# The front of a hand-written list of steps put in another order, with twelve more products of zeros, in a gated-attention and feed-forward kernel

## Chip, cores and metric

The kernel runs on one core of one Trainium2 chip. The metric is the device time of one execution in microseconds (us). Three runs of the kernel before took 465.76, 466.92 and 478.84 us, median 466.92 us.

## What is computed

The first half is a gated linear attention (an mLSTM cell) over 4 batches, 8 heads, 768 time steps and a head size of 40; the second is a feed-forward layer with a piecewise square between two matrix products, over 3072 tokens, 320 model columns and 2048 hidden ones.

```python
for t in range(S):
    m_new = np.maximum(f_gate[:, :, t] + m, i_gate[:, :, t])
    f_stab = np.exp(f_gate[:, :, t] + m - m_new)
    i_stab = np.exp(i_gate[:, :, t] - m_new)
    C = f_stab[:, :, None, None] * C + i_stab[:, :, None, None] * np.einsum('bhd,bhe->bhde', vt, kt)
    n = f_stab[:, :, None] * n + i_stab[:, :, None] * kt
    h_tilde = np.einsum('bhde,bhe->bhd', C, qt)
    y[:, :, t] = o * h_tilde / denom
...
h = x @ w_in
g = np.where(pos, h, np.where(neg, 0.0, (h + beta) ** 2 / (4.0 * beta)))
return (g @ w_out).astype(np.float32)
```

## The kernel before

**Tiles.** Time is cut into six chunks of 128 steps. A block is one chunk of one batch with its 8 heads, 24 blocks in all, numbered n = 4 * chunk + batch; blocks 0 to 3 are the first chunk, which has no state to carry in. Four blocks make one tile of 512 tokens for the feed-forward half, and that half runs in 96 groups (six tiles by 16 slices of 128 hidden columns).

**A block.** `score` (line 668) multiplies keys by queries on TensorE into two PSUM banks, and VectorE multiplies each half with the block's decay matrix. `main` (line 739) multiplies that by the block's values, which GpSimd has scaled by a gate before (`scale1`, line 660, step `v1`), divides, applies the output gate, transposes on TensorE and writes the tile `xh`, `xl`. `carry` (line 717) makes the state that the next chunk needs, from values scaled by another gate (`scale2`, line 711, step `v2`). For the first chunk the decay matrix is built on TensorE: `mask` (line 453) puts a triangle into PSUM and `add` (line 462) adds the running sums `ac` of the gates; `dec` takes the exponential on ScalarE. For blocks 0 to 3, `scale1` and `scale2` write over the block of values that they read (lines 663 to 665, 713).

**Gates.** `sums` scans the first chunk's gates on VectorE, `gtail` and `gex` finish them. For chunks 1 to 4 together, `bmax` scans 512 steps (`m_r`), sends the rows to other partitions through four transfers (`m_b`, line 308), and `bsum`, `btail`, `exps` go on from there.

**Weights.** `W.0`, `W.1`, ... load pieces of `w_in` and `w_out` in turn (line 502); steps `w` convert a piece on ScalarE (`mg`, `win`, `wh`) and VectorE (`win`, `wl`). `mm.g` is the first product of group g, `out`, `outh`, `outl` the second.

**Zeros.** `hot.k` (line 547) is k products of 512 columns of zeros, which nobody reads:

```python
def hot(k):
    out = psum_a()
    for _ in range(k):
        nc.tensor.matmul(out, zeros[:, :P], zeros, start=True, stop=True)
```

**What sets the order.** One list of step names, `STEPS` (line 48), is walked from left to right (lines 920 to 954). Every call of an engine goes through `InOrder` (line 175), which makes each engine execute its instructions in the order of that walk; so nearly all records of the profile bear line 189, and tiles tell them apart. All loads go through one queue, SP's, in the order of the list. PSUM has eight banks, shared by everything (line 543). Where a name stands several times (`score.1 ... score.1`), each mention runs the next part of that step.

Of the kernel before, what the change touches and what calls it, by code (L numbers as in the profile page):

```python
# [48 lines left out]
    "fi.0 mask.1 fb.0 W.0 vv.0 mask.0 hot.2 sums.0 mask.3 qk.1 add.1 hot.2 add.0 qk.2 w.0 w.0 bmax.0 id.0 dec.1.0 "  # L49
    "dec.1.1 dec.0.0 score.1 qk.3 gtail.0 hot.2 hot.2 bmax.0 gex.0 score.1 mask.2 qk.0 add.2 dec.2.0 dec.2.1 vv.2 "  # L50
    "add.3 v.4 dec.3.1 v1.1 dec.3.0 score.1 og.0 W.1 dec.0.1 score.2 main.1 score.0 bsum.0 bsum.0 bsum.0 w.0 "
    "score.3 score.2 score.2 one.0 score.0 v.1 score.0 v1.2 btail.0 w.0 v1.0 sig.0 main.1 btail.0 hot.4 btail.0 "
    "btail.0 w.0 v1.3 main.0 score.3 v.0 main.0 W.2 hot.2 exps.0 main.0 main.1 main.2 hot.2 hot.2 qn.5 A.4 score.3 "
    "v2.4 main.2 main.2 main.0 w.1 v2.1 qk.4 main.0 w.1 cs.0 main.3 main.1 main.2 main.0 W.3 v.5 carry.4 main.3 "
    "main.3 hot.2 v2.0 qn.4 main.1 decs.0 main.1 v.2 w.1 carry.1 main.3 A.5 A.6 main.2 w.2 carry.0 main.2 main.3 "
    "main.3 prep.4 carry.0 w.2 v1.4 prep.4 v2.5 score.4 w.2 prep.4 decs.0 W.4 carry.1 w.3 -- score.4 mm.0 relu.0 "
    "max.0 mm.1 w.2 main.4 w.2 relu.1 main.4 W.5 carry.5 W.6 carry.4 v2.2 w.3 w.3 main.5 main.5 prep.5 prep.5 "
    "score.4 carry.2 carry.2 max.1 mm.3 relu.3 prep.5 mm.2 w.4 carry.5 qk.5 prep.6 main.4 relu.2 main.4 v1.5 max.3 "
    "w.4 w.4 carry.5 prep.6 w.5 qk.6 og.1 max.2 out.0 out.1 out.2 w.5 w.5 w.4 w.4 score.5 so.1 score.5 score.5 A.7 "
    "W.7 score.6 w.6 carry.4 carry.4 v.6 w.6 prep.7 score.6 prep.6 mm.5 w.6 score.6 v1.6 qn.6 sig.1 main.5 main.4 "  # L60
    "main.4 so.2 relu.5 so.2 max.5 main.5 mm.4 relu.4 w.6 main.5 w.6 qn.7 w.7 w.7 prep.7 out.3 main.6 main.6 main.6 "
    "v2.6 carry.6 max.4 mm.6 carry.5 w.7 gh.5 gl.5 carry.6 gh.4 so.3 so.3 v.3 v2.3 carry.3 W.8 outh.4.2.3 carry.6 "
    "w.8 w.8 mm.7 outh.4.0.1 gl.4 main.6 outl.4 outh.5.2.3 A.8 relu.6 carry.3 main.7 A.9 qk.7 score.7 w.8 main.5 "
    "prep.9 relu.7 max.6 max.7 main.6 gh.6 gl.6 W.9 outh.5.0.1 outl.5 outh.6.2.3 outh.6.0.1 w.9 W.10 W.11 outl.6 "
    "w.9 w.9 v.8 main.7 w.8 w.8 v.7 score.7 W.12 prep.7 score.7 w.10 w.10 w.10 qk.9 gh.7 lg.0 main.4 main.4 gl.7 "
    "main.4 mm.9 relu.9 max.9 qn.8 mm.8 v1.7 main.7 carry.6 W.13 w.11 w.11 w.11 v2.7 carry.7 W.14 w.10 w.10 main.6 "
    "relu.8 carry.7 max.8 carry.7 gh.9 outh.7.0.1 main.7 w.12 w.12 w.12 outh.7.2.3 so.4 so.4 mm.11 relu.11 mm.10 "
    "main.8 prep.8 main.7 v.9 w.12 main.5 w.12 outl.7 gh.8 outh.8.0.1 outh.8.2.3 main.5 main.5 gl.8 qn.9 w.13 w.13 "
    "gl.9 mm.12 w.13 relu.10 max.10 max.11 w.14 w.14 so.1 w.14 so.5 so.5 gh.10 relu.12 gl.10 max.12 main.7 outl.8 "
    "outh.9.2.3 qk.8 outh.9.0.1 outl.9 mm.13 relu.13 gh.11 main.8 max.13 w.14 gl.11 w.14 W.15 w.15 outh.10.2.3 "  # L70
    "outh.10.0.1 outl.10 main.6 main.6 main.6 so.6 carry.7 so.6 w.15 w.15 v1.8 og.2 ++ gh.13 qk.10 gh.12 gl.12 "
    "score.8 prep.8 score.8 gl.13 outh.11.0.1 A.10 main.8 main.8 main.7 main.7 main.7 outh.11.2.3 outl.11 mm.15 "
    "relu.15 max.15 outh.12.0.1 outh.12.2.3 outl.12 prep.8 outh.13.2.3 so.7 score.8 main.8 main.8 mm.14 v2.8 "
    "relu.14 max.14 gh.14 mm.17 relu.17 main.9 main.9 mm.16 v2.9 so.7 outh.13.0.1 outl.13 outh.14.2.3 stack.10 "
    "max.17 gh.17 qk.10 score.9 carry.8 stack.10 prep.10 qn.10 gl.14 outh.14.0.1 outl.14 gl.17 prep.9 prep.9 mm.19 "
    "score.9 score.9 carry.8 qn.11 so.0 so.0 carry.8 gh.15 relu.16 max.16 gl.15 relu.19 max.19 v1.9 carry.8 main.9 "
    "qk.11 stack.11 stack.11 A.11 prep.11 qk.12 main.9 main.9 main.8 gh.19 main.8 gl.19 outh.15.2.3 sig.2 stack.10 "
    "stack.10 outh.15.0.1 outl.15 sto.0.1 sto.0.3 gh.16 gl.16 mm.20 relu.20 max.20 qk.11 main.8 main.8 mm.22 "
    "relu.22 max.22 sto.0.2 carry.9 carry.9 mm.18 relu.18 max.18 main.9 mm.25 mm.23 main.10 main.10 prep.10 prep.10 "
    "v.10 relu.25 score.10 score.10 main.9 main.9 outh.16.2.3 v.11 outh.16.0.1 outl.16 outh.17.0.1 qk.12 gh.18 "  # L80
    "gl.18 outh.17.2.3 outl.17 carry.9 sto.0.0 stack.11 outh.18.0.1 score.10 stack.11 v.13 outh.18.2.3 outl.18 "
    "outh.19.2.3 qn.13 main.9 gh.22 prep.11 main.8 max.25 v2.10 carry.10 v1.10 mm.21 main.10 main.8 A.12 main.8 "
    "gh.20 carry.9 gl.20 relu.23 mm.27 main.10 main.10 main.10 A.14 qk.14 carry.10 max.23 outh.19.0.1 outl.19 "
    "outh.20.0.1 outh.20.2.3 relu.21 max.21 gl.22 main.9 gh.21 gl.21 score.11 score.11 main.10 prep.11 score.11 "
    "main.10 main.10 stack.12 stack.12 main.11 mm.24 relu.24 stack.12 v1.11 main.11 main.11 main.11 main.11 max.24 "
    "gh.23 gl.23 qk.13 mm.26 relu.26 max.26 main.11 outl.20 outh.21.0.1 gh.26 main.10 mm.31 relu.31 stack.12 "
    "outh.21.2.3 qn.12 A.13 gh.25 max.31 gh.24 gl.24 stack.14 outl.21 prep.12 prep.12 carry.10 main.9 main.9 v.12 "
    "outh.22.0.1 outh.22.2.3 outl.22 carry.10 qk.13 outh.23.2.3 outh.23.0.1 outl.23 main.11 main.11 mm.29 gl.25 "
    "outh.24.0.1 relu.29 v2.11 outh.24.2.3 main.11 mm.28 main.11 gl.26 outl.24 main.10 carry.11 max.29 qn.14 "
    "relu.27 max.27 gh.31 prep.13 prep.12 outh.25.0.1 outh.25.2.3 outl.25 relu.28 stack.14 main.9 main.10 max.28 "  # L90
    "main.10 gh.27 gl.27 outh.26.0.1 main.11 main.11 main.11 stack.13 v2.12 v1.12 outh.26.2.3 main.12 main.12 "
    "main.12 gh.29 gl.29 main.13 main.13 carry.11 mm.30 score.12 outl.26 outh.27.0.1 score.12 score.12 stack.13 "
    "prep.13 prep.13 stack.13 gl.31 main.12 main.12 gh.28 gl.28 relu.30 mm.35 outh.27.2.3 outl.27 carry.12 "
    "outh.28.0.1 prep.14 carry.11 carry.11 mm.32 outh.28.2.3 outl.28 outh.29.0.1 outh.29.2.3 main.12 main.12 v.15 "
    "outl.29 v1.13 max.30 og.3 prep.14 stack.13 score.13 relu.32 gh.30 qk.15 outh.30.2.3 max.32 gl.30 v2.13 A.15 "
    "prep.14 carry.12 carry.12 main.12 relu.35 qk.14 max.35 gh.35 sig.3 qn.15 gh.32 outh.30.0.1 score.13 g5.5 "
    "score.13 main.13 main.13 main.13 main.13 outl.30 outh.31.0.1 outh.31.2.3 outl.31 stack.15 stack.15 mm.36 "
    "relu.36 v.14 gl.35 mm.33 sto.1.3 carry.13 v2.14 relu.33 max.33 mm.34 carry.12 max.36 gh.33 qk.15 gl.32 mm.39 "
    "main.15 qn.16 carry.13 carry.13 A.16 gl.33 sto.1.0 relu.34 qk.16 main.13 sto.1.1 relu.39 max.34 main.13 g5.5 "
    "carry.13 stack.15 stack.15 mm.41 g5.5 gh.34 outh.32.0.1 outh.32.2.3 outl.32 outh.33.2.3 outh.33.0.1 relu.41 "  # L100
    "max.41 stack.14 gh.36 outl.33 outh.34.2.3 outh.34.0.1 qk.17 prep.15 max.39 prep.15 gh.39 carry.14 mm.38 "
    "relu.38 main.12 gl.36 sto.1.2 gl.34 mm.37 outl.34 outh.35.2.3 outh.35.0.1 main.13 main.13 relu.37 main.15 g5.5 "
    "carry.14 v.18 v1.14 outl.35 outh.36.2.3 outh.36.0.1 main.14 stack.14 score.14 gl.39 main.12 max.37 gh.37 qk.16 "
    "mm.40 mm.43 max.38 qk.17 v2.15 main.14 stack.16 carry.15 main.14 score.14 stack.16 outl.36 score.14 gl.37 "
    "outh.37.2.3 outh.37.0.1 relu.40 outl.37 prep.15 main.14 main.14 relu.43 main.14 max.40 score.15 main.14 max.43 "
    "gh.38 gl.38 score.15 score.15 main.12 carry.14 main.14 stack.17 outh.38.0.1 outh.38.2.3 outl.38 gh.40 gl.40 "
    "main.12 main.12 stack.16 stack.16 prep.16 main.13 main.13 main.13 stack.17 prep.16 v1.15 prep.16 mm.45 g5.5 "
    "carry.14 mm.42 relu.42 mm.47 main.15 outh.39.0.1 main.14 max.42 v.16 gh.41 gl.41 qk.18 main.15 main.15 qn.17 "
    "outh.39.2.3 mm.44 stack.17 outl.39 outh.40.2.3 outh.40.0.1 outl.40 outh.41.2.3 relu.47 main.15 max.47 carry.15 "
# [919 lines left out]
```

## Time and profile before

| | us |
|---|---|
| median of three runs | 466.92 |
| lowest and highest run | 465.76, 478.84 |
| profiled execution, its own time | 465.84 |
| its span in the trace | 464.1 |
| TensorE (PE) busy | 456.0 |
| VectorE (DVE) busy | 350.7 |
| ScalarE (ACT) busy | 327.5 |
| GpSimd (POOL) busy | 144.1 |

The span runs from the first to the last record; the profiled execution's own time is 1.74 us longer. Matmuls are pipelined and the ends of their records are modelled, so a busy TensorE may still be waiting a little: distances between starts are the safer reading. Float32 products stand in the trace as two records each. PEld is TensorE's load of the stationary operand, which runs beside the products. SPq is the queue on which SP issues transfers.

### The profile page before, as it was taken

The numbers are of one execution on the slowest core, as the hardware profiler recorded it, in microseconds if no ns is written. First come the engines' busy times: TensorE is split into PE (matmuls) and PEld (weight loads), VectorE is DVE, ScalarE is ACT, GpSimd is POOL, SyncE is SP. The second block draws the span as 40 slices with busy tenths as digits, with TensorE's granted clock in tenths as the row PEclk, the third lists the DMA queues.
The fourth block names the chain that finished last, engine by engine and source line by source line (L and its number), as shares of the span: only waits on it lengthen the run. The fifth ranks groups of instructions, "written<-read, shape, count | busy, mean of one in ns | idle before, by whom it ended". The sixth has DMA issues, their size and how long they took to land.

```text
span 464.1 us, 8795 instructions
## 1 busy us (share of the span) xinstructions
PE 456.0 (98%) x3333; PEld 408.5 (88%) x3336; DVE 350.7 (76%) x625; ACT 327.5 (71%) x593; POOL 144.1 (31%) x153
## 2 busy tenths in 40 slices
PE   6999999999999999999999999999999999999996
PEld 3888789998899999999988899989988898989986
DVE  5786789998979889878999988786775985443523
ACT  3679999998985586877777666766777734464651
POOL 2364233212543624423425643433213231000000
PEclk9999999999999999999999999999999999999999
DMA  6899959726445442564165437234616000010001
GB/s 215 291 283 352 296 175 347 220 67 166 147 115 148 118 132 91 171 177 124 48 177 161 118 89 203 63 78 155 159 57 160 1 1 0 2 42 16 1 0 57
DMA packets 23048, 60.60 MB, mean 131 GB/s; under 512 B 2599, under 2 KB 9535, under 8 KB 23007
## 3 DMA queue, kind: packets, MB, share of 16 engines
q1 hardware_dynamic: 22719, 59.81, 43.2%
q8 instruction: 26, 0.43, 0.4%
q10 hardware_dynamic: 288, 0.25, 0.2%
q14 instruction: 15, 0.12, 0.1%
HBM read 55.96 MB, written 4.01 MB: 129 GB/s over the span
## 4 chain that ended last, share of the span: by engine, by line
PE 87%; DVE 4%; ACT 3%; DMA 3%; issue 1%; SPq 1%; DVEq 0%
PE ps L189 87%; DMA qs<-in_qs 1%; DMA ident<-in_cst 1%; ACT r L189 1%; DVE stk L189 1%; SPq L189 1%; DVE hv L189 1%; DVE r L189 1%; DVE gl L189 0%; ACT Abc L189 0%; ACT raw L189 0%; ACT win L189 0%; ACT mg L189 0%; DVE win L189 0%; DVE xl L189 0%
## 5 line engine op out<-in xcount | busy, mean ns | idle before, releaser
L189 PE MATMUL ps<-oh,gh 128*128 128x320 f32 x368 | 112.3, 315 | 0.1
L189 PE MATMUL ps<-ow,gh 128*128 128x320 f32 x368 | 110.1, 309 | 0.0
L189 PE MATMUL ps<-xh,wh 128*128 128x512 f32 x288 | 100.6, 403 | 0.1
L189 PE MATMUL ps<-xh,wl 128*128 128x512 f32 x288 | 98.2, 395 | 0.0
L189 ACT ACTIVATE r<-ps,half 128x512 f32<-128x512 f32 x96 | 65.6, 683 | 44.5 <-PE ps L189 39.4
L189 DVE SCALAR_TENSOR_TENSOR r<-ps,r 128x512 f32<-128x512 f32 x96 | 64.7, 685 | 39.0 <-ACT r L189 38.7
L189 DVE TENSOR_TENSOR gl<-r,gh 128x512 fp32r<-128x512 f32 x92 | 69.9, 769 | 25.7 <-ACT gh L189 24.7
L189 ACT CAST gh<-r 128x512 fp32r<-128x512 f32 x92 | 56.2, 617 | 46.4 <-PE ps L189 21.6
L189 PEld LDWEIGHTS ps<-oh,gh 128*128 128x128 f32 x368 | 69.1, 188 | 1.9 <-issue 0.3
L189 PEld LDWEIGHTS ps<-ow,gh 128*128 128x128 f32 x368 | 69.2, 188 | 1.3
L189 PE MATMUL ps<-oh,gl 128*128 128x320 f32 x368 | 70.2, 311 | 0.0
L189 PEld LDWEIGHTS ps<-xh,wl 128*128 128x128 f32 x288 | 54.1, 188 | 12.8
L189 ACT ACTIVATE r<-r 128x512 f32<-128x512 f32 x96 | 60.7, 633 | 3.0
L189 PE MATMUL ps<-xl,wh 128*128 128x512 f32 x192 | 60.3, 395 | 0.0
L189 PEld LDWEIGHTS ps<-oh,gl 128*128 128x128 f32 x368 | 58.1, 188 | 1.1
L189 PEld LDWEIGHTS ps<-xh,wh 128*128 128x128 f32 x288 | 50.3, 188 | 7.8 <-DVE Abc L189 0.2
L189 ACT ACTIVATE Abc<-Abc,nA 128x128 f32<-128x128 f32 x160 | 50.4, 391 | 0.1
L189 POOL TENSOR_TENSOR v<-vk,G 128x328 f32<-128x328 f32 x36 | 28.9, 807 | 53.2 <-DMA vk<-in_vk 28.2
L189 POOL TENSOR_TENSOR y<-y,z 128x320 f32<-128x320 f32 x24 | 21.1, 882 | 76.2 <-DVE y L189 76.2
L189 PEld LDWEIGHTS ps<-xl,wh 128*128 128x128 f32 x192 | 36.0, 188 | 8.8
L189 POOL TENSOR_TENSOR m<-m 128x1024 bf16<-128x1024 f32 x16 | 31.6, 1976 | 37.6 <-DVE m L189 35.0
L189 DVE SCALAR_TENSOR_TENSOR stk<-raw,ident,qs 120x1024 fp32r<-120x1024 f32 x28 | 37.9, 1356 | 2.9 <-ACT raw L189 2.8
(143 smaller groups left out, 665.4 us busy)
## 6 DMA issues: line engine op xcount, KB each, us to landing
qs<-in_qs SPq DMA_DIRECT2D x28, 480.0 KB
Abc<-a_d SPq DMA_DIRECT2D x20, 512.0 KB
vk<-in_vk SPq DMA_DIRECT2D x20, 324.0 KB
wraw<-in_w_in SPq DMA_DIRECT2D x8, 768.0 KB
wraw<-in_w_out SPq DMA_DIRECT2D x8, 640.0 KB
sig<-in_og SPq DMA_DIRECT2D x6, 640.0 KB
qn<-in_qn SPq DMA_DIRECT2D x20, 180.0 KB
raw<-in_qk SPq DMA_DIRECT2D x20, 160.0 KB
```

The source lines that it names most:

```text
L189: r = getattr(self.engine, name)(*args, **kwargs)
```

## The change

Only `STEPS` changes, in its first 204 names (210 after it); the other 1417 names are the same in the same order. Every name of the old front stands in the new one equally often, but for `hot.2`, which stands six times more often: the products of zeros go from 20 to 32. The list is one line longer, so line 189 becomes 190. The first line before and after:

```diff
 STEPS = (
-    "fi.0 mask.1 fb.0 W.0 vv.0 mask.0 hot.2 sums.0 mask.3 qk.1 add.1 hot.2 add.0 qk.2 w.0 w.0 bmax.0 id.0 dec.1.0 "
...
+    "vv.0 hot.4 hot.2 hot.2 mask.1 fi.0 mask.0 mask.3 hot.2 v.0 sums.0 id.0 add.0 dec.0.0 dec.0.1 mask.2 qk.3 add.3 "
+    "fb.0 bmax.0 add.2 dec.2.0 dec.2.1 add.1 dec.1.0 gtail.0 gex.0 qk.0 score.0 score.0 qk.1 score.1 dec.3.1 "
+    "dec.3.0 qk.2 score.3 score.1 bmax.0 bsum.0 score.2 W.0 v2.0 og.0 v1.1 vv.2 dec.1.1 score.1 hot.2 W.1 main.1 "
...
 )
```

So eight products of zeros now stand first on TensorE; the value blocks `vv.0` and `v.0` and all four transfers of queries and keys (`qk`) of the first chunk stand ahead of the first piece of `w_in`; the masks and sums of all four blocks are done before the first score; and `carry.0` comes before `main.0`, with `v.0` loaded and `v2.0` done ahead of `v1.0`. With that order `v1.0` scales the block of values which `v2.0` has already scaled, where before each had a block loaded for it; the instructions and their sizes are the same.

SP's queue at the start of the program, before (`fi`, `fi_r`, `fi_b`: gates; `wraw`: weights; `ow`: value blocks; `raw`: queries and keys, each block in two transfers; `ident`: constants):

```order
1 L186 DMA fi_128<-in_fi 96x256
2 L189 DMA fi_r<-in_fi 32x2x512
3 L189 DMA fi_b<-in_fib 128x256
4 L189 DMA wraw<-in_w_in 128x1536
5 L189 DMA ow<-in_vk 128x2x328
6 L189 DMA raw<-in_qk 40x2x512 x2
7 L189 DMA raw_200<-in_qk 40x2x512 x2
8 L189 DMA ident<-in_cst 128x154
9 L189 DMA raw_224<-in_qk 40x2x512 x2
10 L189 DMA m_b<-m_r 32x129 x4
```

The same queue in the changed kernel:

```order
1 L187 DMA ow<-in_vk 128x2x328
2 L190 DMA fi_146<-in_fi 96x256
3 L190 DMA ow<-in_vk 128x648
4 L190 DMA ident<-in_cst 128x154
5 L190 DMA raw_199<-in_qk 40x2x512 x2
6 L190 DMA fi_r<-in_fi 32x2x512
7 L190 DMA fi_b<-in_fib 128x256
8 L190 DMA raw<-in_qk 40x2x512 x4
9 L190 DMA raw_279<-in_qk 40x2x512 x2
10 L190 DMA m_b<-m_r 32x129 x4
11 L190 DMA wraw<-in_w_in 128x1536
```

The first weights went from fourth to eleventh place, behind `m_b`; the first gates stand behind a value block, and three blocks' queries and keys stand between `fi_r` and `m_b`.

GpSimd, from the first gate copies on, before (`ow_141` holds the values of blocks 0 and 1, `ow_268` those of 2 and 3; `y` belongs to `main`):

```order
17 L189 TENSOR_TENSOR ow_141<-ow_141,G_117 128x328
18 L189 COPY fi_r_135<-ident_92 128x320
19 L189 TENSOR_TENSOR ow_268<-ow_268,G_117 128x328
20 L189 TENSOR_TENSOR ow_141<-ow_141,G_117 128x328
21 L189 TENSOR_TENSOR ow_268<-ow_268,G_117 128x328
22 L189 TENSOR_TENSOR y_396<-y_396,z_379 128x320
```

And after (`ow_161` is the block that `v.0` loads, scaled in row 17 for `carry.0` and in row 20 for `main.0`; `ow_128` holds block 1):

```order
17 L190 TENSOR_TENSOR ow_161<-ow_161,G_117 128x328
18 L190 TENSOR_TENSOR ow_128<-ow_128,G_117 128x328
19 L190 COPY fi_r_212<-ident_92 128x320
20 L190 TENSOR_TENSOR ow_161<-ow_161,G_117 128x328
21 L190 TENSOR_TENSOR ow_317<-ow_317,G_117 128x328
22 L190 TENSOR_TENSOR y_425<-y_425,z_391 128x320
```

Row 20 now writes over what `carry.0` reads on TensorE, so it stands behind `carry.0`, and `main.0` stands behind it.

ScalarE at the start, before (`Abc`, `A_169`: decay matrices; `mg`, `win`: conversion of the first weights; `G`: gates):

```order
1 L186 ACT_TABLE_LOAD
2 L186 ACTIVATE mg<-wraw 128x768
3 L189 ACTIVATE win<-wraw 128x768
4 L189 ACTIVATE Abc<-ps 128x512 x3
5 L189 ACTIVATE G<-ps 128x128
6 L189 ACTIVATE Abc<-ps 128x512 x2
```

And after:

```order
2 L187 ACTIVATE Abc<-ps 128x512
3 L190 ACTIVATE Abc<-ps 128x512 x4
4 L190 ACTIVATE G<-ps 128x128
5 L190 ACTIVATE A_153<-ps 128x512 x2
6 L190 ACTIVATE Abc<-ps 128x512
7 L190 ACTIVATE mg<-wraw 128x768
8 L190 ACTIVATE win<-wraw 128x768
```

The conversion went from ahead of the decay matrices to behind them.

## Rows read from the trace of the kernel before

**Rows 1.** The page, busy time of each engine over the span.

```profile
PE 456.0 (98%) x3333; PEld 408.5 (88%) x3336; DVE 350.7 (76%) x625; ACT 327.5 (71%) x593; POOL 144.1 (31%) x153
```

**Rows 2.** Timeline of TensorE: start, length, what, [idle before, what ended it].

```profile
2.18 0.58 PE L186 MATMUL ps<-late_t,idb 128*128 128x512 bf16 x1 [2.18 <-POOL rst L186]
2.56 1.49 PE L189 MATMUL ps<-late_t,idb 128*128 128x512 bf16 x3
3.84 1.06 PE L189 MATMUL ps<-zeros 128*128 128x512 bf16 x2
...
5.59 0.39 PE L189 MATMUL ps<-ac,pick 96*128 96x128 bf16 x4
...
7.58 0.38 PE L189 MATMUL ps<-less,ac 96*128 96x512 bf16 x1
9.02 0.46 PE L189 MATMUL ps<-raw 40*128 40x128 f32 x2 [1.07 <-DMA raw<-in_qk]
9.96 1.13 PE L189 MATMUL ps<-raw 40*128 40x128 f32 x14 [0.48 <-DMA raw<-in_qk]
...
12.07 0.30 PE L189 MATMUL ps<-ident,ex 128*128 128x128 f32 x1 [0.23 <-DMA ident<-in_cst]
```

**Rows 3.** The same timeline, further on.

```profile
15.60 1.98 PE L189 MATMUL ps<-ow,Abc 128*128 128x41 f32 x16
17.51 2.06 PE L189 MATMUL ps<-raw 40*128 40x128 f32 x32
19.50 1.04 PE L189 MATMUL ps<-zeros 128*128 128x512 bf16 x3
20.37 1.88 PE L189 MATMUL ps<-ow,Abc 128*128 128x41 f32 x16
22.07 0.60 PE L189 MATMUL ps<-zeros 128*128 128x512 bf16 x2
```

**Rows 4.** The same timeline, where both orders meet.

```profile
51.42 2.06 PE L189 MATMUL ps<-raw 40*128 40x128 f32 x32
```

**Rows 5.** Timeline of VectorE.

```profile
2.80 0.48 DVE L189 TENSOR_TENSOR_SCAN m<-fi,m 96x128 f32<-96x128 f32 x1 [1.88 <-DMA fi<-in_fi]
...
4.93 0.60 DVE L189 TENSOR_TENSOR ac<-ac 64x128 f32<-64x128 f32 x2
...
6.68 1.27 DVE L189 TENSOR_TENSOR_SCAN m_r<-fi_r,m_r 32x512 f32<-32x512 f32 x1
...
9.19 0.14 DVE L189 COPY carry<-m_r 32x1 f32<-32x1 f32 x1
11.01 1.29 DVE L189 TENSOR_TENSOR Abc<-ps,Abc 128x512 f32<-128x512 f32 x2 [1.67 <-PE ps L189]
14.75 0.62 DVE L189 TENSOR_TENSOR fi_b<-fi_b,m_b 128x128 f32<-128x128 f32 x2 [2.46 <-DMA m_b<-m_r]
```

**Rows 6.** Timeline of ScalarE.

```profile
6.95 0.90 ACT L186 ACTIVATE mg<-wraw 128x768 f32<-128x768 f32 x1 [4.93 <-DMA wraw<-in_w_in]
7.75 0.86 ACT L189 ACTIVATE win<-wraw 128x768 int32<-128x768 uint16 x1
```

**Rows 7.** Timeline of GpSimd.

```profile
0.73 0.52 POOL L186 MEMSET zeros<- 128x512 bf16 x1 [0.29 <-POOLq L1018]
...
12.82 0.73 POOL L189 TENSOR_TENSOR ow<-ow,G 128x328 f32<-128x328 f32 x1 [3.89 <-issue]
```

**Rows 8.** The chain that ended last, in order of time: start, length, what.

```profile
41.41 0.70 ACT r L189
...
53.52 82.05 PE ps L189 x574
```

**Rows 9.** Windows: PE, PEld, DVE, ACT, POOL busy; clock; DMA share, GB/s.

```profile
2.00:3.00 1.00, 0.82 (x3) 0.26 (x3) 0.20 (x1) 0.01 (x1) 0.54 (x4) 1.00 0.48 127
...
9.00:10.00 1.00, 0.50 (x4) 0.36 (x4) 0.30 (x2) 1.00 (x3) 0.00 (x0) 1.00 0.67 212
...
20.00:30.00 10.00, 9.95 (x83) 9.08 (x84) 8.78 (x30) 6.29 (x11) 4.57 (x7) 1.00 1.03 317
```

223 rows, old and new, of the table STEPS are left out of this document.

## The prediction, made before the changed kernel was run

> **What bounds the kernel now.** I read the page first: TensorE is busy 98% of the span, 456.0 of 464.1 us, and no other engine over 76% [rows 1]. Then the chain of waits: from 53.52 us on it runs through TensorE for 82 us in one piece; between 41.41 and 53.51 us it runs through ScalarE and a little VectorE [rows 8]. So the kernel is TensorE's list of products, one after the other, and only its front has holes. The two orders meet again on TensorE at the scores of blocks 5 and 6, which start at 51.42 us [rows 4]; from there every engine's order is the old one, give or take a few instructions. A shift of that start is a shift of the end, if ScalarE keeps pace. So the question is: when does that product start in the changed kernel?
>
> Up to there, the timeline of TensorE shows four kinds of loss. It starts at 2.18 us, when GpSimd has made the masks. Its first products are slow: three masks take from 2.56 to 3.84 us, 0.427 us each, which for 512 columns is 1.2 GHz; from 5.59 us on four zeros take 0.87 us, 0.218 us each, which is 2.4 GHz [rows 2, 3]. (The granted clock reads 1.00 even from 2 to 3 us [rows 9], so I take the level from the lengths.) Then it waits for queries and keys: the last sum ends about 7.80 us (7.58 + 0.22), the transposition of the gates starts at 12.07 us, and in the 4.27 us between there are one block's scores (1.00 us, half of 17.51 to 19.50 us) and four zeros (0.87 us): 2.40 us are lost. And there are small waits hidden in "busy": `main.1` takes from 15.60 to 17.51 us, 1.91, where the next one takes 20.37 to 22.07, 1.70: 0.2 us [rows 2, 3].
>
> **What the change removes and adds.** Useful products are the same. Zeros: 12 more at 0.218 us, +2.6 us, since TensorE has no hole left to put them in unless something is late. (The first eight products are cold in both orders; that they are now zeros and not masks changes nothing in their number.) Start: zeros need only the memset, which ends at 1.25 us (0.73 + 0.52) [rows 7]; with 0.15 us to begin, the first product comes at 1.40 us, -0.8 us. The hole of 2.40 us goes, and the 0.2 us of `main.1`. Without new waits: 2.6 - 0.8 - 2.4 - 0.2 = -0.8 us.
>
> **New waits: the queue of loads.** SP's loads land in the order of the queue, as the rows show. The first gates (96 KB) are there at 2.80 us and `w_in`, 1120 KB into the queue, at 6.95 us [rows 5, 6]: 1024 KB in 4.15 us, 247 KB/us. A half of a q and k transfer (160 KB) takes 9.96 - 9.02 = 0.94 us [rows 2]. As a test: from 9.96 us two more halves and 77 KB of constants end at 9.96 + 1.88 + 0.31 = 12.15 us; TensorE had the constants at 12.07 [rows 2]. Block 3's two halves then end at 14.0 us, and `m_b`, behind them, was there at 14.75 [rows 5]: 0.7 us later.
>
> Now the new queue. The first gates stand behind 328 KB: 2.80 + 1.33 = 4.13 us. `v.0` and the constants (401 KB): 5.75. Block 3's halves: 7.63. The 128 KB of `fi_r`: 8.15, of `fi_b`: 8.67. Blocks 0, 1 and 2: 10.55, 12.43 and 14.3. `m_b`: 15.0. The first weights (768 KB more, at 247 to the 317 KB/us of 20 to 30 us [rows 9]): 17.4 to 18.1 instead of 6.95.
>
> At one point here the Trainium skill bears. The row first: while only q and k move, the share of busy transfer engines is 0.67 at 212 GB/s, from 9 to 10 us [rows 9]. The page "DMA: Bandwidth & Descriptors", section "Why a DMA increments its semaphore by 16 and not by 1", states that a transfer runs on the largest number of engines, up to 16, that divides the outer sizes on both sides; 40 rows would mean ten engines of 16, and the 0.67 of the trace, near ten sixteenths, agrees. It speaks against the change: eight such halves ahead of the 16-engine weights leave six engines with little to do. By it a half would cost 160 KB at ten sixteenths of 247 KB/us, 1.04 us for 0.94, and `m_b` would come 0.8 us later; the sum below would be 0.8 us more.
>
> **New waits on TensorE, in its order.** I follow it by starts.
> - Eight cold zeros from 1.40 us: 4.82; six masks and two zeros at 0.218: 6.56. `add.0` needs `ac`: the scan started at 2.80 and `ac` was done at 5.53 (4.93 + 0.60) [rows 5]; the same 2.73 us from 4.13 give 6.86, and with 0.06 us to begin (5.53 to 5.59) 6.92. **Wait 0.36.**
> - Four sums at 0.88 (5.59 to 7.80 us holds two of them and two zeros) and one pair of masks (0.44): 10.88 us. The gates' transposition needs `fi_r`, its scan and the tail (6.68 to 9.19 us, 2.51 [rows 5]): 8.15 + 2.51 = 10.66. No wait. Block 0's scores start at 11.0, its keys were there at 10.55. Block 1's second half lands at 12.43, and TensorE is ready at 12.0: **wait 0.43.** Three blocks at 1.00 and two zeros: 15.87 us.
> - `main.1` now needs a multiplication on VectorE (0.65 us [rows 5]) that stands behind `fi_b<-fi_b,m_b` (0.62 us), and that waits for `m_b`: 15.0 + 1.3 + 0.1 = 16.4. **Wait 0.53.** Behind the waiting instruction stand all later multiplications of scores, so every `main` after it would wait with it.
> - `carry.0` ends, and `main.0`, next but nothing on TensorE, needs `v1.0`, which must wait for `carry.0`, because it writes over its values: 0.73 us on GpSimd [rows 7] and 0.1 for the two signals (0.06 us was one of them above). **Wait 0.83.** Behind `v1.0` on GpSimd stand `v1.2` and the first `y`; four zeros and two behind `main.0` give them time.
>
> Followed in the same way, no later product up to the scores of blocks 5 and 6 finds its input missing, though some only just. New waits: 0.36 + 0.43 + 0.53 + 0.83 = 2.1 us. Sum: -0.8 + 2.1 = **+1.3 us**. Profiled time 465.84 + 1.3 = 467.1 us. The median of the runs shown is 466.92, 1.08 us above the profiled execution, the lowest run 465.76, 0.08 below it; I take the sum as it is, 467.1 us.
>
> **Bounds.** Each wait can be nothing: 465.84 - 0.8 = 465.0 us, and less by small waits inside "busy" like that of `main.1` that don't come back. Above, the loads: `m_b` came 0.7 us after the place that the queue gave it; if the first gates and block 1's keys also come 0.7 us later than I put them, the end comes up to 1.4 us later, 468.5 us. ScalarE's side is a rival, below. The loads' cover is the 12 zeros: where a load is late by less than the zeros ahead of it, it costs nothing.
>
> **Rivals.**
> 1. *The waits don't come.* If the queue serves small transfers beside large ones, the first gates and `m_b` are early, and only `v1.0` is left: -0.8 and at most 0.83 us: 465.0 to 465.9, say 465.4 us. For it: transfers of later queues overlap when issued early. Against: the constants landed at 12.07 us, just where the order of the queue puts them [rows 2].
> 2. *ScalarE becomes the bound, and the kernel slower.* Before, `mg` and `win` of the first weights (0.90 + 0.86 us) ran at 6.95 us, in a wait of 4.93 us [rows 6]. Now they run after 17.3 us, and the chain passes through ScalarE from 41.41 to 53.51 us anyway [rows 8]. If no later idle time takes them up, 1.76 us come on top: 465.84 + 1.3 + 1.76 = 468.9 us. It decides from the point at which the first weights land so late that ScalarE has less than 1.76 us of idle time left before 41 us. Against: from 20 to 30 us alone it is idle for 3.7 of 10 us [rows 9], after the weights' new landing.
> 3. *The zeros pay for themselves.* If the clock fell back in the old holes, the zeros would save more than they cost; but the sums and scores after 5.59 us run at the length of 2.4 GHz through all holes [rows 2, 3], so the zeros buy nothing: no change of the sum.
>
> **How the numbers follow.** The forecast, +1.3 us, has 0.45; rival 1 has 0.3, rival 2 0.2, and 0.05 is left for rival 3 and what I don't see. The lower two of the runs shown lie 1.2 us apart, so a median may be that much off. Range 464.0 to 469.5 us, one microsecond below rival 1's lower end and a little above rival 2. About 2%, 9 us, is what a measurement of this kernel tells from no change; no case comes near it: faster 0.01, same 0.97, slower 0.02.
>
> **What would show it.** Right: the first product of zeros at 1.4 us and full rate from about 4.8 us; the first sum near 6.9 us; a wait before `main.1` that ends with a VectorE multiplication behind `m_b`; a wait of 0.8 us before `main.0`, ended by GpSimd; the scores of blocks 5 and 6 at about 52.7 us, and from there the same distances as before. Wrong: `m_b` well before 15 us, those scores before 51 us or after 54, or a chain that runs through ScalarE past 60 us.

## The result and the profile after

The changed kernel takes 470.79 us (median of 4 executions, 469.46 to 472.50), the kernel before 466.34 us in the same comparison: a ratio of 1.0103, 95% interval 1.0082 to 1.0123. (A few executions of several of these kernels take some per cent longer, one of the four of the kernel before among them, at 478.84 us; the ratios leave them out.) The kernel is slower by less than 2%, with an interval clear of 1, and outside the predicted range of 464.0 to 469.5 us. The profiled execution took 471.88 us, its span is 470.1 us (before: 465.84 and 464.1). The four executions come in two pairs: 469.46 and 469.71 us with a mean granted clock of TensorE of 0.996, 471.88 and 472.50 us with 0.992. What lies behind the clock is part of the result, below.

The page, as [rows 1], then the clock in 40 slices of the span and the chain that ended last:

```profile
span 470.1 us, 8817 instructions
...
PE 461.8 (98%) x3348; PEld 412.0 (88%) x3348; DVE 350.4 (75%) x625; ACT 327.6 (70%) x593; POOL 143.0 (30%) x153
...
PEclk9979999999999999999999999999999999999999
...
PE 95%; DMA 2%; DVE 1%; SPq 1%; issue 0%; POOL 0%; ACT 0%; DVEq 0%; POOLq 0%
```

The clock of the kernel before:

```profile
PEclk9999999999999999999999999999999999999999
```

TensorE is busy 98% of the span as before, so the shares say nothing. The third digit of the clock, a 7 for about 23.5 to 35 us, does: before, all forty digits are 9. Where did the 6.0 us come from? The row that answers to [rows 4]:

```profile
57.50 2.06 PE L190 MATMUL ps<-raw 40*128 40x128 f32 x32
```

51.42 has become 57.50: all of the 6.0 us stand there already, and from there to the end it is the old distance (412.6 us, before 412.7). So the loss lies in the front. Its first part, TensorE's timeline in the columns of [rows 2]:

```profile
1.31 0.61 PE L187 MATMUL ps<-zeros 128*128 128x512 bf16 x1 [1.31 <-POOL zeros L187]
1.72 3.19 PE L190 MATMUL ps<-zeros 128*128 128x512 bf16 x7
4.70 1.70 PE L190 MATMUL ps<-late_t,idb 128*128 128x512 bf16 x6
...
7.11 0.39 PE L190 MATMUL ps<-ac,pick 96*128 96x128 bf16 x4 [0.28 <-DVE ac L190]
...
11.61 0.30 PE L190 MATMUL ps<-ident,ex 128*128 128x128 f32 x1 [0.35 <-ACT Abc L190]
11.85 4.24 PE L190 MATMUL ps<-raw 40*128 40x128 f32 x64
16.02 0.60 PE L190 MATMUL ps<-zeros 128*128 128x512 bf16 x2
16.46 1.88 PE L190 MATMUL ps<-ow,Abc 128*128 128x41 f32 x16
...
20.66 0.90 PE L190 MATMUL ps<-ow 128*120 128x123 f32 x6 [1.46 <-DVE Abc L190]
22.49 3.64 PE L190 MATMUL ps<-ow,Abc 128*128 128x41 f32 x16 [0.94 <-POOL ow L190]
25.93 1.91 PE L190 MATMUL ps<-zeros 128*128 128x512 bf16 x4
```

Up to `main.1` at 16.46 us the times of the forecast hold (1.4, 4.82, 6.92 and 16.4 us). The waits for queries and keys of [rows 2] are gone. Then come two waits: `carry.0`, the row of six products at 20.66 us, waits 1.46 us for a multiplication on VectorE, and `main.0` waits 0.94 us for `v1.0` on GpSimd. The `main.0` behind them takes 25.93 - 22.49 = 3.44 us; the same product took 22.07 - 20.37 = 1.70 us in [rows 3]. Windows of the stretch, with TensorE's busy time, granted clock, DMA share and GB/s:

```profile
18.00:20.00 2.00, 1.20 (x7) 1.00 1.05 401
20.00:22.00 2.00, 0.90 (x6) 1.00 1.02 355
...
23.00:29.00 6.00, 6.00 (x25) 0.50 0.92 291
29.00:30.00 1.00, 1.00 (x10) 0.97 1.02 403
```

After four microseconds in which TensorE worked for 2.1, its clock is at 1.2 GHz, and it stays there for more than 6 us, in which the trace shows TensorE busy throughout. In distances between starts (hot ones from the run called banks_own below, 21.18 to 22.92 us): `main.0` 3.44 for 1.70, four zeros 1.71 for 0.87, four transpositions 0.85 for 0.44, two zeros 0.72 for 0.43: 3.3 us.

Why does `carry.0` wait for VectorE, which makes none of its inputs? VectorE's timeline:

```profile
15.51 0.62 DVE L190 TENSOR_TENSOR fi_b<-fi_b,m_b 128x128 f32<-128x128 f32 x2 [0.55 <-DMA m_b<-m_r]
16.04 0.68 DVE L190 TENSOR_TENSOR Abc<-ps,Abc 128x512 f32<-128x512 f32 x1
...
17.68 0.68 DVE L190 TENSOR_TENSOR Abc<-ps,Abc 128x512 f32<-128x512 f32 x1
18.28 0.42 DVE L190 TENSOR_TENSOR_SCAN fi_r<-rst,fi_b 128x128 f32<-128x128 f32 x1
...
19.85 0.15 DVE L190 TENSOR_TENSOR dc_b<-fi_r 128x1 f32<-128x1 f32 x1
19.92 1.28 DVE L190 TENSOR_TENSOR Abc<-ps,Abc 128x512 f32<-128x512 f32 x2
```

The pool `ps` has eight tiles, PSUM's eight banks, and a block's scores hold two of them until VectorE has multiplied them by their decay (`Abc<-ps,Abc`). Block 2's two multiplications stand behind six small operations of the gates (18.28 to 19.92 us), and these behind `m_b`, which landed at 15.5 us. The first multiplication is done at about 20.6 us, and `carry.0` starts. The chain of waits, in order of time (start, length, what), tells the same story without a gap:

```profile
12.05 3.38 DMA m_b<-m_r
...
15.51 0.30 DVE fi_b L190
...
20.01 0.61 DVE Abc L190
...
20.66 0.91 PE ps L190 x6
...
21.70 0.75 POOL ow L190
...
22.49 17.56 PE ps L190 x117
```

### The profile page after: what moved, and what is told of

Its sections match the earlier page's. It is cut to its first block, busy times and chain, and to the rows that moved or that the text cites. A ratio compares the mean times of both kernels' runs of the same rounds, so it can differ in the third digit from the quotient of the medians.

```text
span 470.1 us, 8817 instructions
## 1 busy us (share of the span) xinstructions
PE 461.8 (98%) x3348; PEld 412.0 (88%) x3348; DVE 350.4 (75%) x625; ACT 327.6 (70%) x593; POOL 143.0 (30%) x153
## 4 chain that ended last, share of the span: by engine, by line
PE 95%; DMA 2%; DVE 1%; SPq 1%; issue 0%; POOL 0%; ACT 0%; DVEq 0%; POOLq 0%
PE ps L190 95%; DMA fi_r<-in_fi 1%; SPq L190 1%; DMA m_b<-m_r 1%; DVE Abc L190 0%; DVE m_r L190 0%; DVE fi_r L190 0%; DVE fi_b L190 0%; POOL ow L190 0%; DVE m_b L190 0%; SPq L187 0%; ACT r L190 0%; DVE fi L190 0%; DVE dc_b L190 0%; DVEq L190 0%
```

## The experiments

Theory 1: two waits, one of them for a bank of PSUM, and the clock that falls behind them. Rival A: the added zeros are paid for. Rival B: the later loads set the pace. Rival C, for the first wait: its cause is another. Times are medians of the executions that the ratio compares; the ratio and its 95% interval are against executions of the kernel before on the same chip (medians 466.05 to 466.24 us). "Fell" counts the compared executions whose mean clock is 0.996 or less (the traces of the changed kernel, own, zeros_first and before_lean show the fall itself); the kernel before has such ones too, 16 of 91, at 467.3 to 469.6 us.

| run | time, us | ratio | fell | range of the others, us |
|---|---|---|---|---|
| changed kernel | 470.79 | 1.0103 [1.0082, 1.0123] | 4 of 4 | |
| own | 467.69 | 1.0045 [1.0022, 1.0068] | 5 of 12 | 466.72 to 467.80 |
| own_late | 468.81 | 1.0052 [1.0033, 1.0070] | 9 of 12 | 466.79 to 467.50 |
| fill | 468.64 | 1.0052 [1.0032, 1.0071] | 0 of 6 | 467.75 to 469.11 |
| zeros_first | 466.08 | 1.0000 [0.9985, 1.0016] | 4 of 12 | 465.16 to 466.39 |
| banks | 467.37 | 1.0029 [1.0009, 1.0048] | 3 of 9 | 466.70 to 467.72 |
| banks_own | 465.79 | 0.9985 [0.9973, 0.9996] | 0 of 12 | 465.36 to 466.31 |
| banks_own_lean | 469.38 | 1.0072 [1.0044, 1.0100] | 8 of 8 | |
| before_lean | 470.52 | 1.0088 [1.0061, 1.0115] | 6 of 6 | |
| trim_tail | 465.12 | 0.9998 [0.9970, 1.0026] | 2 of 11 | 464.83 to 465.67 |
| trim_mid | 464.81 | 0.9964 [0.9951, 0.9977] | 0 of 9 | 464.36 to 465.19 |
| trim_half | 464.58 | 0.9957 [0.9939, 0.9974] | 0 of 11 | 464.18 to 465.87 |
| before_trim | 465.66 | 0.9996 [0.9983, 1.0009] | 0 of 10 | 465.11 to 467.49 |

**Only the clock: fill.** The changed kernel with zeros through both waits.

```diff
-    ... main.1 hot.2 hot.2 bsum.0 ... v.1 score.2 main.0 ...
+    ... main.1 hot.2 hot.9 bsum.0 ... v.1 score.2 hot.4 main.0 ...
```

> The changed kernel with eleven zeros more and nothing else: seven ahead of the wait of `carry.0` (1.5 us for its 1.46), four ahead of that of `main.0` (0.87 us for its 0.94). Both waits stay, TensorE only works on zeros through them. Theory 1: the clock stays at 2.4 GHz in 23 to 29 us, the 3.3 us of slow products go and the waits stay: 470.8 - 3.3 = 467.5 us. If the clock has no part in it (the waits alone, or later loads), 470.8 to 471. Rival A (zeros are paid for one by one): 470.8 + 11 x 0.218 = 473.2.

Measured 468.64 us, 2.15 below the changed kernel and 1.1 above what theory 1 gave, with eleven products more, and the clock at 0.999 or 1.000 in all six executions. Its windows, then its timeline:

```profile
18.00:20.00 2.00, 2.00 (x12) 1.00 1.05 419
20.00:22.00 2.00, 1.92 (x14) 1.00 1.05 373
22.00:26.00 4.00, 4.00 (x33) 1.00 0.89 228
```

```profile
17.42 2.55 PE L189 MATMUL ps<-zeros 128*128 128x512 bf16 x11
19.81 0.80 PE L189 MATMUL ps<-ow 128*120 128x123 f32 x6
...
21.54 1.98 PE L189 MATMUL ps<-ow,Abc 128*128 128x41 f32 x16
```

The waits still are there, only as zeros; the clock holds, and `main.0` takes 1.81 us (the row behind it starts at 23.35). As the cause of the loss, rival A is out: eleven zeros made the kernel faster.

**One wait at a time: own, banks, own_late.** In own, `v2.0` scales the block which `v.0` loads and `v1.0` the one which `vv.0` loaded, each once, as in the kernel before (in the changed kernel `v1.0` scales again what `v2.0` has scaled, so that `main.0` there multiplies values scaled by both gates, which the kernel before and the runs built on own do not):

```diff
-        t["v"] = v[:, :H * D1].rearrange("p (h d) -> p h d", d=D1)
+        t["w" if n < B else "v"] = v[:, :H * D1].rearrange("p (h d) -> p h d", d=D1)
...
-        nc.gpsimd.tensor_tensor(out=v2, in0=t["v"], ...
+        nc.gpsimd.tensor_tensor(out=v2, in0=t["v" if n >= B else "w"], ...
```

> The changed kernel, but block 0's values are scaled out of and into the block in which they were loaded, as in the kernel before, so that this scaling on GpSimd no longer waits for the first `carry.0` product; that product's own wait for VectorE stays. Theory 1 (the loss is two new waits between 19 and 22.5 us, and the clock that falls to 1.2 GHz behind them until about 29 us): the wait of `main.0` goes (0.94 us); if one wait of 1.46 us is not enough to bring the clock down, the 3.3 us of slow products go as well: 470.8 - 0.9 - 3.3 = 466.6 us; if it still falls, 469.9. Rival A (the twelve added zeros cost 0.218 us each somewhere): 470.8 - 0.9 = 469.9 at best, the clock in 23 to 29 us no matter. Rival B (loads that come later set the time of blocks 1 to 3, so that a wait which goes at 22 us comes back at the next load): 470.8.

> As the run in which block 0's values stay in their own block, and `carry.0` stands behind the next `main.0` besides, so that its product no longer holds up the queue at 19.2 us. Theory 1: `main.0` needs a bank of PSUM in `carry.0`'s place; if it finds one, both waits go: 470.8 - 0.9 - 1.5 - 3.3 = 465.1 us; if the bank that is given back last is what the queue waits for, whoever asks for it, the 1.46 us stay with `main.0` and the time is that of the run without the move, 466.6 or 469.9. Rivals A and B: 468.4 to 470.8.

In own, the wait of `main.0` is gone and that of `carry.0` stays, 1.41 us in its trace. With this one wait the clock fell in 5 of 12 executions (468.82 to 472.16 us) and held in 7 (median 467.32, 0.7 us above what theory 1 gave for that). Own_late is the same with `carry.0` taken behind `main.0`:

```diff
-    ... score.0 carry.0 btail.0 btail.0 v1.0 btail.0 btail.0 v.1 score.2 main.0 score.2 ...
+    ... score.0 btail.0 btail.0 v1.0 btail.0 btail.0 v.1 score.2 main.0 carry.0 score.2 ...
```

TensorE's timeline then has the wait in front of `main.0`:

```profile
17.68 1.03 PE L189 MATMUL ps<-zeros 128*128 128x512 bf16 x4
19.90 1.95 PE L189 MATMUL ps<-ow,Abc 128*128 128x41 f32 x16 [1.19 <-DVE Abc L189]
```

Whoever comes first waits for the bank; the move gains nothing (468.81 us, and the clock fell in 9 of 12). Banks changes VectorE's order alone:

```diff
-    ... score.0 carry.0 btail.0 btail.0 v1.0 btail.0 btail.0 v.1 score.2 main.0 score.2 w.0 ...
+    ... score.0 score.2 score.2 carry.0 btail.0 btail.0 v1.0 btail.0 btail.0 v.1 main.0 w.0 ...
```

> The changed kernel with one move on VectorE alone: block 2's two multiplications of scores by their mask-and-decay, which read two banks of PSUM, stand right behind block 0's second one and ahead of the last six small operations of the gates. Theory 1 (`carry.0` waits for a bank that block 2's scores hold, and VectorE gives it back late because the small operations stand ahead): the 1.46 us hole goes, `carry.0` starts at about 19.2 us; `main.0` still waits for GpSimd behind it, about 0.9 us. If that one wait leaves the clock up: 470.8 - 1.5 - 3.3 = 466.0 us, else 469.3. Rival C (`carry.0` waits for something else that ends at 20.6 us, its values or its load): no change, 470.8.

Its VectorE, then its TensorE:

```profile
17.21 1.88 DVE L189 TENSOR_TENSOR Abc<-ps,Abc 128x512 f32<-128x512 f32 x3
```

```profile
19.02 0.80 PE L189 MATMUL ps<-ow 128*120 128x123 f32 x6
20.75 1.98 PE L189 MATMUL ps<-ow,Abc 128*128 128x41 f32 x16 [0.94 <-POOL ow L189]
```

Three multiplications in a row, and `carry.0` follows its zeros without a wait. Its wait was for block 2's multiplications, which make none of its inputs and give back banks; rival C is out. With the clock up (6 of 9) the median is 467.09 us, 1.1 above what theory 1 gave and 1.5 below that of fill, where both waits stand.

**Both waits away: banks_own.** Banks and own together.

> That move, and block 0's values scaled out of and into the block in which they were loaded, so that `main.0` does not wait for `carry.0`. Theory 1: both holes go, TensorE has no idle time of more than 0.4 us behind 12 us, and the clock stays at 2.4 GHz in every execution: 470.8 - 1.5 - 0.9 - 3.3 = 465.1 us, and no execution above 466.5. Rival A (the twelve added zeros are paid for whatever the waits): at least 1 us above the kernel before, 467.1 or more.

Measured 465.79 us, no execution above 466.31 or with a mean clock below 0.999: as theory 1 has it, but for 0.7 us, and slightly faster than the kernel before. Rival A (467.1 or more) is out, and so is rival B: loads come as late as in the changed kernel (ScalarE starts on the first weights at 18.11 us, 17.16 there), and nothing comes back. The timeline:

```profile
17.97 1.03 PE L189 MATMUL ps<-zeros 128*128 128x512 bf16 x4
18.84 0.79 PE L189 MATMUL ps<-ow 128*120 128x123 f32 x6
19.47 1.88 PE L189 MATMUL ps<-ow,Abc 128*128 128x41 f32 x16
21.18 1.03 PE L189 MATMUL ps<-zeros 128*128 128x512 bf16 x4
22.05 0.27 PE L189 MATMUL ps<-ident,fi_b 128*128 128x128 f32 x1
```

The medians with the clock up add up: 465.79 us without waits; +1.3 with that of `main.0` alone (banks, 467.09), +1.5 with that of `carry.0` alone (own, 467.32), +2.8 with both (fill, 468.64); and the clock makes it 470.79.

**What zeros are for: before_lean, banks_own_lean, zeros_first.** The first two lose every `hot` of the list from 15 us on, the kernel before twelve products, banks_own 22. Zeros_first is the kernel before with `hot.4 hot.2 hot.2` put ahead of its list.

> The kernel before without its last twelve products of zeros (from 19.5 us on), 2.6 us of TensorE. With zeros fully paid for: 466.1 - 2.6 = 463.5 us. If they only fill waits: 465.5 to 466.1; if the holes that open bring the clock down: 468 to 470.

> The same without its last 22 products of zeros (from 15 us on; the first ten stay), 4.8 us of TensorE at 2.4 GHz. Theory 1 with the zeros fully paid for: 465.1 - 4.8 = 460.3 us. If the zeros stand where their neighbours must wait anyway (for VectorE's and ScalarE's steps of the blocks, or for the split weights), the time turns into idle time and little changes: 463 to 465; and if such holes bring the clock down, 466 to 469.

> The kernel before with eight zeros more ahead of all its products, as the changed kernel has them, and nothing else. Theory 1: TensorE starts on them 0.8 us earlier, they delay the first masks and sums by less than the 2.40 us that TensorE then waits for queries and keys, and nothing is late behind that: 466.3 us, within 0.4. Rival A (zeros are paid for): 8 x 0.427 or 0.218 us less the 0.8 us of the earlier start, 467.2 to 468.9. If instead it is faster by more than 0.5 us, TensorE's clock rises earlier there than in the kernel before.

Without its last twelve zeros the kernel before takes 4.3 us more. Its windows:

```profile
20.00:22.00 2.00, 1.80 (x15) 1.00 1.06 418
22.00:24.00 2.00, 2.00 (x18) 0.88 1.03 379
...
26.00:36.00 10.00, 10.00 (x49) 0.50 1.04 319
36.00:38.00 2.00, 2.00 (x19) 0.70 0.96 352
```

The clock fell in 22 to 24 us, ahead of the one larger wait:

```profile
21.87 0.33 PE L188 MATMUL ps<-ident,m_b 128*128 128x128 f32 x1 [0.20 <-DVE m_b L188]
...
25.09 0.90 PE L188 MATMUL ps<-ident,y 128*128 128x128 f32 x3 [0.54 <-POOL y L188]
25.78 3.48 PE L188 MATMUL ps<-ow,A 128*128 128x41 f32 x16
```

Only 0.2 us of idle time stand ahead of the fall; then TensorE is busy for ten microseconds at 1.2 GHz (this `main` takes 3.28 us, the row behind it starts at 29.06). Banks_own without its zeros ends at 469.38 us, with a mean clock of 0.982 to 0.989. In both, the last of the three cases came, by 0.5 and 0.4 us worse than I had put it; what the zeros are worth is the clock.

Zeros_first answers as expected: eight zeros in front cost nothing. Its profiled execution shows more, a fall of the clock behind the old waits for queries and keys:

```profile
8.00:10.00 2.00, 1.15 (x9) 1.00 0.70 227
...
12.00:14.00 2.00, 2.00 (x8) 0.50 0.63 171
```

That execution took 467.54 us, the ones with the clock up 465.16 to 466.39. The kernel before has the same waits, and 16 of its 91 executions have as low a mean clock; that this is the same fall is likely, but I have no trace of one.

**Which zeros are too many: the trims.** From banks_own, trim_mid takes two zeros at each of the places with four (17.97, 21.18 and 24.62 us), trim_tail the last four (29.8 and 32.4 us), trim_half all ten. Before_trim takes two zeros at each of two places with four from the kernel before.

```diff
-    ... main.1 hot.2 hot.2 bsum.0 ... sig.0 hot.2 hot.2 main.0 ... w.0 hot.2 main.0 main.0 hot.2 main.0 ...
+    ... main.1 hot.2 bsum.0 ... sig.0 hot.2 main.0 ... w.0 main.0 main.0 hot.2 main.0 ...
```

> The same kernel without six zeros between 17 and 25 us, two at each of the three places where four stand (ahead of `carry.0`, ahead of the transposition of the gates, ahead of the first transposed rows). Paid for: 465.8 - 1.3 = 464.5 us. The waits that open behind them (VectorE's banks, GpSimd's rows): 465.3 to 465.8. If the clock falls in some executions, as in the kernel without any of these zeros: those at 468 or more, the others at 464.5.

> The kernel with both waits taken away (465.8 us), without its last four products of zeros, two ahead of the last `main.0` products' neighbours at 29.8 us and two right ahead of the first weight products at 32.4 us. If zeros are paid for where TensorE is never idle and the clock stays: 465.8 - 4 x 0.218 = 464.9 us. If they cover a wait for transposed rows or split weights: 465.8. If the clock falls behind them: 467 or more.

> Both: ten zeros fewer, as many late zeros as the kernel before has (twelve). All paid for and the clock up: 465.8 - 10 x 0.218 = 463.6 us, 2.5 us below the kernel before; with a wait opening at 18 or 25 us, 464.1 to 464.9; with the clock down in some executions, 467 or more for these.

> The kernel before with two zeros fewer at each of the two places where four stand (ahead of `main.0` at 19.5 us and ahead of the first transposed rows at 24.7 us): eight late zeros instead of twelve. It tells whether the gain of the kernel with six zeros fewer (464.8 us) needs the new order or only the shorter list. If zeros are paid for and the clock stays: 466.2 - 4 x 0.218 = 465.3 us, and up to 0.3 more where GpSimd's rows are then late. If the clock falls in a part of the executions behind the two waits for queries and keys that this kernel still has: those at 468 or more, the median at 466 or above.

Trim_mid takes 464.81 us, 1.0 below banks_own and 0.4% faster than the kernel before. Four of its six zeros were paid for (0.87 us by their length); the last two only covered a wait for GpSimd, which its trace now shows, 0.2 us longer than they were (from `main.1` to the second row below it is 8.57 us, in banks_own 9.24):

```profile
23.21 0.39 PE L189 MATMUL ps<-zeros 128*128 128x512 bf16 x1
24.29 0.55 PE L189 MATMUL ps<-ident,y 128*128 128x128 f32 x3 [0.69 <-POOL y L189]
```

Trim_half is no better beyond its interval: 0.2 us for four more zeros. Trim_tail is unclear: 464.83 to 465.67 us in nine executions, 470.41 and 470.82 in two with a mean clock of 0.989. That its four zeros are what kept the clock up is not shown: trim_half lacks them too, and its clock held in all eleven. Before_trim shows no change clear of noise, so a shorter list alone, tried at two places of the old order, does not give the gain of trim_mid. Trim_mid is the version I would keep.

## Why the prediction was wrong

- **Start, cold zeros, first sums: right.** 1.31 us for 1.40, 4.70 for 4.82, 7.11 for 6.92. The first gates' scan came at 4.33 us for 4.13. (No row gave the 0.15 us from the memset to the first product; it took 0.05 us.)
- **`main.1`: the right time by luck.** It started at 16.46 us for 16.4, but the wait of 0.53 us behind `m_b` did not come: TensorE goes from the scores through two zeros to `main.1` without a gap, and `main.1` starts before the multiplication behind `m_b` has ended (16.04 + 0.68 us; only its second four heads need it). It was late for other reasons. The transposition of the gates started 0.7 us later than I put it; 0.35 us of this is a wait that ends with ScalarE's `Abc`, none of its inputs either, so most likely a bank as well. And 64 products of scores took 4.17 us from start to start for 4 x 1.00. In fill they took 3.78 us (11.50 to 15.28), so the wait of 0.43 us for keys is probably in there, in pieces.
- **The rule on DMA:** by that of the Trainium skill ("DMA: Bandwidth & Descriptors", "Why a DMA increments its semaphore by 16 and not by 1") I had estimated that `m_b` would come 0.8 us later than 15.0. VectorE used it at 15.51 us, between queue and rule; but in fill and trim_mid, whose queue is the same up to there, at 14.33 and 14.32 us, without waiting for it. The runs differ among themselves by more than the rule would make, and decide nothing on it; the 15.0 us of the queue's order hold to 0.7 us.
- **`main.0` behind `v1.0`: right.** 0.94 us for 0.83 in the trace, 1.3 us in the times.
- **"No later product [...] finds its input missing": the step that failed.** It followed inputs, and `carry.0` had all of its own. What it had not was a place to write. I counted instructions in VectorE's queue behind `m_b` for `main.1` alone and stopped there; block 2's multiplications stand in the same queue, and the banks come free with them. Price: 1.5 us.
- **Rival 3, "the zeros pay for themselves", dismissed: the larger miss.** The sum put the clock at nothing. I argued from one execution, in which the clock had held through the old holes; in the profiled one of zeros_first it fell behind them. The changed kernel has 2.1 us of work in the 4 us before the fall, and pays 3.3 us in the profiled execution, 2.1 us between the medians of fill and the changed kernel. And zeros pay for themselves in the kernel before, too: 4.3 us.
- **Sum.** Predicted +1.3 us, measured +4.5 (470.79 - 466.34), or +4.7 over the 466.1 us of the kernel before in the experiments. Without the two waits and the clock the new order gains some 0.3 us (465.79 for 466.1), where my first terms had come to +0.5, the 0.53 us of `main.1` among them. The waits of 1.3 and 1.5 us and the clock's 2.1 us make the rest, to 0.1 us.
- **Why 3.3 and 2.1 us of clock:** the median of 470.79 us lies between the two pairs of executions, and the profiled one is of the slower pair: 471.88 - 468.64 = 3.2 us. The expectations of the runs took the 3.3 us off the median, which is why those for fill, own, banks and banks_own are 0.7 to 1.1 us too low. Taken off 471.9 they give 468.6, 467.7, 467.1 and 466.2 us, for 468.64, 467.32, 467.09 and 465.79.
- **Rivals 1 and 2: out.** The first gates and `m_b` were not early, and the scores of blocks 5 and 6 came at 57.50 us, behind the 54 us that I had named as a sign of being wrong. ScalarE converts the first weights at 17.16 us, about as foreseen, and the chain of the changed kernel is 95% TensorE.

## What to carry to other kernels

When an order is remade, follow for each product three things, not one: its inputs, its place to write (which reader frees the next bank, and what stands ahead of that reader in its queue), and whose data it writes over. An operation that waits for a late transfer holds up all that is queued behind it, the releases of buffers included; here moving two multiplications ahead of six small operations was worth 1.5 us and more. Zeros in the list are to be judged by the clock they keep and not by their length: try them out one place at a time, over ten executions and not one, since a clock that falls now and then shows in some of them alone. A cost that is read from one profile belongs to that execution, and is to be set against its own time and not against the median.

## What was not expected of the hardware

- The clock fell without any long idle time: the waits ahead of it were 1.46 and 0.94 us in the changed kernel and 0.20 us in before_lean. It then stayed at 0.50 for 6 us in the one and for more than 10 us in the other, in which TensorE was busy throughout. What the chip goes by there, these runs do not tell. The Trainium skill ("Perfetto Trace Analysis", "Matmul Optimizations") states that the engine scales its power with its use and that products should come back to back in batches. Fill agrees (clock 1.000, 2.15 us less); before_lean shows that TensorE busy by the trace is not yet enough to have the clock back.
- The same program has it fall in some executions and not in others: 5 of 12 in own, 9 of 12 in own_late, 0 of 12 in banks_own. A single profile of own_late (clock 0.998, 466.79 us) would have told of a kernel nearly as good as the one before; by all its executions it is 0.5% slower.
- The Trainium skill ("Perfetto Trace Analysis", "Optimization Strategy") states that consistent bubbles, the same gap repeating on the engine that should be saturated, can mean that SBUF or PSUM has no room for the next tile. Here a single gap of 1.46 us was of that kind, and the releaser's name in the row, an instruction that makes none of the product's inputs, was the sign.
